# A gated recurrence and a gated long convolution on one core: the same 2430 operations, issued from another order table

## The chip, the core and the metric

The kernel runs on one core of a Trainium2 chip. A core has five engines that each work through their own list of instructions in order: TensorE (PE, matmuls; its weight loads are shown as PEld), VectorE (DVE), ScalarE (ACT), GpSimd (POOL) and SyncE (SP). In this kernel SP does no arithmetic: it issues every DMA. The engines meet only at semaphores, so an instruction whose input or buffer is not ready holds up everything behind it on its own engine.

The metric is the device time of one execution in microseconds (us). Of the kernel before there are three runs: 461.68, 462.61 and 464.66 us, median 462.61.

## What is computed

Four sequences of 6272 steps with 256 channels go through a gated recurrence, and its result through a gated long convolution with a learned filter. Cut to what matters:

```python
def _attn_ref(x, f_logit, lower_bound):
    sig = 1.0 / (1.0 + np.exp(-f_logit))
    f = lower_bound[None, None, :] + (1.0 - lower_bound[None, None, :]) * sig
    i = 1.0 - f
    h = np.zeros((B, D), dtype=np.float32)
    for t in range(S):
        h = f[:, t] * h + i[:, t] * x[:, t]
        y[:, t] = h
    return y

def _moe_ref(x, w_proj, filter_fft, w_out):      # x is the y of above
    proj = x @ w_proj
    x1, x2, x3 = (proj[..., :D].copy(), proj[..., D:2 * D].copy(), proj[..., 2 * D:].copy())
    X2 = np.fft.rfft(x2, n=S, axis=1)
    H = np.fft.rfft(filter_fft, n=S, axis=0)[None, :, :]
    x2_conv = np.fft.irfft(X2 * H, n=S, axis=1)
    y = x1 * x2_conv * x3
    return y @ w_out
```

Batch is 4, S is 6272 = 49 * 128, D is 256; inputs and output are float32.

## The kernel before

The kernel is written as a recording and a replay. The code walks through the computation once and records 2430 operations with `plan.op`: for each one its kind, the engines that may do it (the keys of its cost), the function that issues it, and what it reads and writes. `Plan.emit` then issues them in the order and on the engine that a constant string, `ORDER`, lists. Three characters of that string are one entry: a number in base 64 whose low three bits choose PSUM banks, whose next three bits name the engine (`ENGINES`; MUL is VectorE doing the copy and the following product in one instruction), and whose rest is the operation's number. "A0g", for example, is 3360 = 52 * 64 + 4 * 8 + 0: operation 52, on SP. The planner that made the table is not part of the kernel. The costs, the transfer times `dma` and `lag` and the constant `MARGIN = 1.0` that stand in the calls of `op` are what it is told; they are not read at run time.

The work falls into these stages. The names are the kinds of the operations, the lines are those of the profile.

- Start, once. The filter is loaded in 13 pieces (`ff`, L610), copied (`fr`), turned by TensorE (`rot`, L621), copied (`f2`) and taken through a two-step Fourier transform (`FF1` L646, `afs`, `FF2` L664, `hw`). The spectrum H is stored to DRAM (`hst`, L673). Dummy matmuls (`warm`, L591) stand where the table puts them. The first recurrence runs alongside.
- Recurrence of one batch (`hgrn`), 13 chunks of 512 steps. `load` (L321) brings 512 KB of f_logit into FL and 512 KB of x into XT; there are NX = 3 buffers of each. Then `sig` (L324, ACT), `u` (L326, POOL), and for each half of the channels `su` (L338, transposes on PE), `f` (L351 on ACT or L353 on DVE), `scan` (L359, DVE) into HA, and `wrap`: a copy of a part of HA to another part, 128 KB for a full chunk, on POOL (L293), ACT (L281) or as a DMA on SP (L291).
- P stage: TensorE projects HA (`P`, L705), and `x2` copies the result into X2, on ACT (L281) or DVE (L286).
- Spectrum of one batch, 16 units: `F1` (L718), `A` (copy to HA's other part), every fourth unit `mini` (L734) and `zm` (L740), `F2` (L777), then two products with the spectrum, either directly out of PSUM on DVE (`prod`, L798) or as a copy (L281) and a product on POOL (`pm`, L807), `slot` (L782, POOL), and back: `I2` (L817) and `Th` (copy). The piece of H that a unit needs is loaded by `H` (L755) into one of NH = 3 buffers, unless it is still there.
- Gate: `x13` (L387, PE) projects HA once more. `xs` copies the result to x1s (ACT L283, DVE L288) and x3s (ACT L281, DVE L286), and `z` multiplies them on POOL (L417), or DVE multiplies directly out of PSUM (L408).
- Output: `I1` (L851, PE), `y` (L857, DVE), `proj` (L869, PE), `o` (copy to one of NO = 3 buffers osb, ACT L283 or DVE L288) and `store` (L879).

The table interleaves these: while the spectrum and the output of one batch run, gate work of the same batch and the recurrence of the next batch stand between them. A P stage needs the whole recurrence of its batch, and the first `F1` needs the whole P stage. So TensorE's list has a repeating shape: a P stage of some 13 us, then a long mixed stage of some 85 us from the first `F1` (L718) of a batch to the first `P` (L705) of the next.

The copies out of PSUM may run on ACT or DVE (`either`); the table chooses one of them for each. This is the loop that replays it:

```python
            word = a * 4096 + b * 64 + c
            yield word // 64, self.ENGINES[word // 8 % 8], word % 8
...
        for i, e, b in self.order():
            o = self.ops[i]
            assert e in o["cost"] and i not in seen and o["preds"] <= seen
...
            o["fn"](*args)
```

## Time and profile before

| | before |
|---|---|
| three runs, us | 461.68, 462.61, 464.66 |
| span of the profiled execution, us | 460.2 |
| VectorE busy | 412.1 us, 90% |
| ScalarE busy | 402.7 us, 88% |
| GpSimd busy | 310.2 us, 67% |
| moved by DMA | 121.40 MB, 264 GB/s on average |

The profile is of one execution. Its page begins with the busy time of each engine, then shows the span in 40 slices of 11.5 us, in tenths of busy time. The granted TensorE clock is at 90% or more in all slices but the second:

```profile
DVE  8689998899999996998999996999999987999872
ACT  6799988799999997899999988999998868989663
POOL 6889766188999643778898435789996603857400
PEclk9899999999999999999999999999999999999999
```

The dips of DVE and POOL are the P stages. Transfers are read in the list of DMA issues; its last column is the median time from issue to landing in us:

```profile
Hu<-H SPq DMA_DIRECT2D x55, 512.0 KB, 4.4
FL<-in_f_logit_dram SPq DMA_DIRECT2D x48, 512.0 KB, 5.4
XT<-in_x_dram SPq DMA_DIRECT2D x48, 512.0 KB, 5.5
out_dram<-osb SPq DMA_DIRECT2D x48, 512.0 KB, 4.3
```

Two cautions for reading it. The ends of matmuls are modelled, so a busy TensorE is not a TensorE at its peak. And an engine's instructions overlap: on ACT and DVE the next one starts a little before the profile shows the end of the last one, so what an instruction costs its engine is the distance from its start to the next start, where nothing idles between them.

### The profile page before, as it was taken

The numbers are of one execution on the slowest core, as the hardware profiler recorded it, in microseconds if no ns is written. First come the engines' busy times: TensorE is split into PE (matmuls) and PEld (weight loads), VectorE is DVE, ScalarE is ACT, GpSimd is POOL, SyncE is SP. The second block draws the span as 40 slices with busy tenths as digits, with TensorE's granted clock in tenths as the row PEclk, the third lists the DMA queues.
The fourth block names the chain that finished last, engine by engine and source line by source line (L and its number), as shares of the span: only waits on it lengthen the run. The fifth ranks groups of instructions, "written<-read, shape, count | busy, mean of one in ns | idle before, by whom it ended". The sixth has DMA issues, their size and how long they took to land.

```text
span 460.2 us, 14622 instructions
## 1 busy us (share of the span) xinstructions
PE 439.7 (96%) x6009; PEld 344.3 (75%) x6009; DVE 412.1 (90%) x471; ACT 402.7 (88%) x582; POOL 310.2 (67%) x293
## 2 busy tenths in 40 slices
PE   7799989999989999999999999999999999999997
PEld 5677778766756889778667889767768897777786
DVE  8689998899999996998999996999999987999872
ACT  6799988799999997899999988999998868989663
POOL 6889766188999643778898435789996603857400
PEclk9899999999999999999999999999999999999999
DMA  8967898986997997386887996579869830756176
GB/s 333 390 268 288 315 307 283 349 284 219 309 353 250 358 315 276 139 246 218 307 300 280 318 317 239 214 248 318 255 235 315 306 138 13 230 200 205 57 287 275
DMA packets 44242, 121.40 MB, mean 264 GB/s; under 512 B 4240, under 2 KB 6672, under 8 KB 44176
## 3 DMA queue, kind: packets, MB, share of 16 engines
q1 hardware_dynamic: 44176, 120.47, 74.0%
q8 instruction: 47, 0.77, 0.7%
q14 instruction: 19, 0.16, 0.1%
HBM read 87.69 MB, written 31.98 MB: 260 GB/s over the span
## 4 chain that ended last, share of the span: by engine, by line
PE 63%; DVE 12%; ACT 11%; DMA 5%; issue 5%; POOL 2%; SPq 0%; DVEq 0%; ACTq 0%; POOLq 0%
PE PS L387 14%; PE PS L817 8%; PE PS L869 7%; PE PS L338 7%; PE PS L705 6%; PE PS L777 6%; PE PS L718 5%; DVE HA L359 5%; PE PS L851 4%; DMA FL<-in_f_logit_dram 3%; DVE ys L857 2%; DVE X L286 2%; ACT FL L324 2%; PE PS L646 2%; ACT fTs L351 1%
## 5 line engine op out<-in xcount | busy, mean ns | idle before, releaser
L326 POOL TENSOR_TENSOR XT<-XT,FL 128x1024 f32<-128x1024 f32 (+1 forms) x52 | 116.9, 2251 | 50.3 <-ACT FL L324 41.9
L359 DVE TENSOR_TENSOR_SCAN HA<-fTs,HA,PS 128x512 f16<-128x512 f32 (+1 forms) x96 | 112.5, 1200 | 2.8 <-ACT fTs L351 1.7
L798 DVE TENSOR_TENSOR PP<-PS,Hu 98x1008 f16<-98x1008 f32 x87 | 101.3, 1197 | 3.4 <-ACT HA L281 1.4
L387 PE MATMUL PS<-HA,W 128*128 128x490 f16 (+1 forms) x416 | 100.4, 367 | 0.9 <-DVE X L286 0.4
L807 POOL TENSOR_TENSOR PP<-HA,Hu 98x1008 f16<-98x1008 f16 x41 | 86.2, 2107 | 1.7 <-PE PS L817 1.0
L281 ACT CAST HA<-PS 128x1024 f16<-128x1024 f32 (+1 forms) x94 | 77.0, 849 | 5.1 <-PE PS L718 3.4
L417 POOL TENSOR_TENSOR zt<-x1s,x3s 128x490 f16<-128x490 f32 (+1 forms) x43 | 52.3, 1222 | 41.8 <-ACT x3s L281 22.9
L857 DVE TENSOR_TENSOR ys<-PS,zt 128x1024 fp32r<-128x1024 f32 (+1 forms) x52 | 58.5, 1149 | 9.5 <-PE PS L851 5.0
L283 ACT ACTIVATE osb<-PS 128x1024 f32<-128x1024 f32 (+1 forms) x51 | 49.9, 992 | 13.9 <-PE PS L869 11.2
L351 ACT ACTIVATE fTs<-PS,nomc 128x512 f32<-128x512 f32 (+1 forms) x89 | 58.3, 679 | 3.7 <-PE PS L338 2.3
L387 PEld LDWEIGHTS <-W 128*128 128x128 f16 x416 | 35.4, 97 | 31.7 <-issue 5.4
L869 PE MATMUL PS<-Wo,ys 128*128 128x256 f32 x392 | 57.7, 292 | 1.3 <-DVE ys L857 1.1
L283 ACT ACTIVATE x1s<-PS 128x490 f32<-128x490 f32 (+1 forms) x92 | 53.5, 594 | 5.0 <-PE PS L387 3.0
L817 PEld LDWEIGHTS <-PP 98*128 98x128 f16 x1024 | 48.7, 98 | 10.6 <-issue 3.1
L324 ACT ACTIVATE FL<-FL 128x1024 f32<-128x1024 f32 (+1 forms) x52 | 53.0, 1026 | 2.2 <-DMA FL<-in_f_logit_dram 2.1
L869 PEld LDWEIGHTS PS<-Wo,ys 128*128 128x128 f32 x392 | 49.4, 188 | 5.8 <-DVE ys L857 2.2
L817 PE MATMUL PS<-VA,PP 98*128 98x98 f16 x512 | 52.2, 207 | 1.5 <-ACT x1s L283 0.8
L817 PE MATMUL PS<-VB,PP 98*128 98x98 f16 x512 | 51.9, 207 | 0.0
L281 ACT CAST Th<-PS 128x784 f16<-128x784 f32 x58 | 48.2, 830 | 2.6 <-PE PS L817 1.6
L338 PE MATMUL PS<-iden,FL 64*128 64x64 f32 x784 | 44.8, 230 | 1.6 <-DVE HA L359 0.9
L705 PE MATMUL PS<-W,HA 128*128 128x256 f16 x392 | 44.4, 273 | 1.0 <-ACT X L281 1.0
L705 PEld LDWEIGHTS <-HA 128*128 128x128 f16 x392 | 42.9, 142 | 1.9 <-issue 1.3
(113 smaller groups left out, 724.3 us busy)
## 6 DMA issues: line engine op xcount, KB each, us to landing
Hu<-H SPq DMA_DIRECT2D x55, 512.0 KB, 4.4
FL<-in_f_logit_dram SPq DMA_DIRECT2D x48, 512.0 KB, 5.4
XT<-in_x_dram SPq DMA_DIRECT2D x48, 512.0 KB, 5.5
out_dram<-osb SPq DMA_DIRECT2D x48, 512.0 KB, 4.3
X<-in_moe_filter_fft_dram SPq DMA_DIRECT2D x9, 512.0 KB, 7.1
H<-Hu SPq DMA_DIRECT2D x4, 512.0 KB, 6.2
Hu<-in_moe_filter_fft_dram SPq DMA_DIRECT2D x2, 512.0 KB, 9.8
H<-Hu SPq DMA_DIRECT2D x4, 256.0 KB, 6.5
```

The source lines that it names most:

```text
L281: nc.scalar.copy(dst, src)
L283: nc.scalar.activation(dst, src, AF.Copy, scale=scale)
L326: op("u", {"POOL": 0.1 + 0.553 * nb}, lambda e, xt=xt, ft=ft: nc.gpsimd.tensor_tensor(xt, xt, ft, op=AOP.mult), r=[("ft", k)], w=[("xt", k)])
L338: nc.tensor.transpose(bank(pb)[:, at[p] + j:at[p] + hn:nb], src[ps, j, cols], iden[ps, ps])
L359: nc.vector.tensor_tensor_scan(h, fT, bank(pb)[:, 512 - hn:512 + hn], init, op0=AOP.mult, op1=AOP.add),
L387: nc.tensor.matmul(PS[:, p, 0:n], W13[:, kh, js], HA[:, HB[kh] + t0:HB[kh] + t0 + n], start=(kh == 0), stop=(kh == 1))
L705: nc.tensor.matmul(pp[:, r - r0, :], column(HB[kh], q_of(r)), W2[:, kh, :], start=(kh == 0), stop=(kh == 1))
L798: nc.vector.tensor_tensor(pr, px.unsqueeze(1).broadcast_to([TB, 2, UE, 63]), hh, op=AOP.mult)
L807: nc.gpsimd.tensor_tensor(pr, spec[:, o, :, 1:64].unsqueeze(1).broadcast_to([TB, 2, UE, 63]), hh, op=AOP.mult)
L817: nc.tensor.matmul(PS[:, ib + o, pr * TB:(pr + 1) * TB], PP[:TB, k, o, n, 2 * pr:2 * pr + 2, :], v[:TB], start=(n == 0), stop=(n == 1))
L857: nc.vector.tensor_tensor(late["ys"][:, yk, :, 0:rn * 128], PS[:, cb:cb + 2, 0:rn * 128], late["zt"][:].rearrange("p k r m -> p k (r m)") ...
L869: nc.tensor.matmul(po[:, i, :], late["ys"][:, yk, kh, i * 128:(i + 1) * 128], Wo[:, kh, :], start=(kh == 0), stop=(kh == 1))
```

## The change

Only the constant `ORDER` differs. The recorded operations, buffers, costs and dependences are the same code; the new table was planned with transfer times that one in ten transfers of the trace exceeds, in place of those in the code. The string is two lines shorter in the file, because its lines are longer, so every line below it moves up by two (L326 becomes L324 and so on). The first lines of both tables:

```diff
 ORDER = (
-    "A0gA1AA5gA6AA+gBDgBIgBNgBSgAAYAOYABIACIAPIApQAdQAzYAqQAoQAkQAyQARIA2QA/YA4AA3AAQAAVYAXYBXgAhSAlSBhgBAQBJYBCAAUIA"
-    "WIAfSBBIA7SBEAAvUBcgBFUBOYBGEBHEAiWBKWBTYBLGBrgBMGBPUBREBYYAnWASABmgA9CA8KBwgBZWBiIBUQBdYBbOBVIBQEBjSBsYBlCBaGAT"
...
+    "AAYA0gA5gAOYABIAnUACIBDgApSA+gAiUBNgAyUBIgAzYAPIAlWBXgBSgAfXAkSAoXAvTAdRBhgA1AA2WA6YAhQARIAQAA7SBEAA/YA9CBFUA4GBwg"
+    "BAQBGEBOYBcgA8CBrgAVYAxTBHMBmgBJAAXYD5gBBIBPTBCAAUIADgBRDBYYBKQA3OBQDEFgBTYATIBMABZTASABaLBUVD6gBiYBLIERgBWFEGgBbL"
...
```

Read entry by entry, the two tables issue the same 2430 operations. On TensorE the order, dummy matmuls aside, is nearly kept: an operation moves by 0.4 places on average and by at most 7 of 738. These counts of operations by engine differ:

| kind | before | after |
|---|---|---|
| xs, copies of the gate | ACT 131, DVE 16, MUL 61 | ACT 121, DVE 27, MUL 60 |
| x2, copies of the P stage | ACT 27, DVE 25 | ACT 30, DVE 22 |
| f2 / afs, copies of the start | ACT 19 / 24, DVE 7 / 8 | ACT 15 / 21, DVE 11 / 11 |
| wrap | POOL 34, ACT 8, SP 6 | POOL 26, ACT 4, SP 18 |
| f / o | ACT 89 / 51, DVE 15 / 1 | ACT 88 / 50, DVE 16 / 2 |
| copies before pm | ACT 39, DVE 2 | ACT 38, DVE 3 |
| A / hw | ACT 55 / 14, DVE 9 / 3 | ACT 56 / 15, DVE 8 / 2 |
| fr | POOL 7, ACT 3, DVE 3 | POOL 8, ACT 3, DVE 2 |

The SP list has 263 operations in place of 251, and the loads, spectrum loads, wraps and stores stand in another order in it. The number of direct products (L798, 87) and of `pm` (L807, 41) is the same; `z` on POOL goes from 43 to 44 after one direct product fewer at L408.

126 lines of the change are left out of this document (62 added, 64 removed).

## The prediction

> **What bounds the kernel now.** The busy shares come first, cut to the stages. I take the long mixed stages from the first L718 of a batch to the first L705 of the next. The columns are start and end, length, then busy us of each engine with its instruction count, granted clock, DMA share and GB/s.
>
> ```profile
> core 0: us, PE busy (x) PEld busy (x) DVE busy (x) ACT busy (x) POOL busy (x), PEclk, DMA share, GB/s
> 88.50:172.70 84.20, 80.16 (x1262) 60.31 (x1260) 79.32 (x88) 79.24 (x118) 68.16 (x54) 1.00 0.87 300
> 185.70:273.00 87.30, 85.92 (x1321) 65.42 (x1320) 84.47 (x91) 82.25 (x124) 66.45 (x57) 1.00 0.79 272
> 285.70:371.40 85.70, 84.83 (x1317) 64.80 (x1315) 83.13 (x90) 81.32 (x124) 68.15 (x57) 1.00 0.75 261
> 432.80:460.20 27.40, 24.08 (x331) 20.94 (x330) 15.49 (x14) 13.20 (x14) 0.00 (x0) 1.00 0.64 256
> ```
>
> No engine is alone. In the long stages PE, DVE and ACT are each busy 94 to 99%; only in the output stage at the end are DVE and ACT half idle. So a change that makes nothing cheaper can win only the few per cent of holes. Who makes the holes is read from the chain that ended last. First its shares by engine (page), then the three pieces after the start-up in which it stands still for a DMA (start us, us, what).
>
> ```profile
> PE 63%; DVE 12%; ACT 11%; DMA 5%; issue 5%; POOL 2%; SPq 0%; DVEq 0%; ACTq 0%; POOLq 0%
> 54.92 5.97 DMA FL<-in_f_logit_dram
> 100.43 6.23 DMA Hu<-H
> 125.69 6.87 DMA FL<-in_f_logit_dram
> ```
>
> The DMA's 5% is 23 us, but a piece of the chain is a latency, not a loss: other engines worked meanwhile. What was lost is in the waits (engine and line, waited for: us in total, times, longest one) and, for the spectrum loads, in the L798 group's idle time after the bar.
>
> ```profile
> POOL XT L326 <- DMA XT<-in_x_dram: 2.4, 3, 1.5
> ACT FL L324 <- DMA FL<-in_f_logit_dram: 2.1, 2, 1.2
> ACT osb L283 <- DMA out_dram<-osb: 1.9, 2, 1.7
> L798 DVE TENSOR_TENSOR PP<-PS,Hu 98x1008 f16<-98x1008 f32 x87 | 101.3, 1197 | 3.4 <-ACT HA L281 1.4 <-DMA Hu<-H 1.0 <-PE PS L777 0.4
> ```
>
> That is all a better-timed table can take from the transfers: L324 and L326 wait at the same two places (near 61 and 133 us), so 2.4 + 1.0 in the run plus 1.9 at the end, 5.3 us or 1.2% of the span.
>
> **Part 1, the transfers.** For each load I counted its cover: the PE work that the table puts between the operation that frees the buffer (or an earlier entry of SP's queue that waits longer) and the first operation that uses the data, each PE group at its median distance to the next start (L387 pair 0.41 us, L705 group 0.87, L718 0.45, L777 0.54, L817 0.70, L338 0.60, L869 1.13). It is compared with the landing times: loads of x and f_logit have median 5.5 and one in ten over 8.8 us; spectrum loads 4.4, one in ten over 6.2, the longest 7.5.
> For x and f_logit the cover's least value goes from 4.4 to 5.1 us, the number under 6.2 from 24 to 10 of 104. Around 61 us the picture is mixed: the f_logit load that was late falls from 7.0 to 5.7, the next pair rises from 5.1 to 7.1 and 9.0. Around 133 us the late pair rises from 5.8 and 6.4 to 6.4 and 8.0.
> For the spectrum loads the least value in batch 0 goes from 3.5 to 5.6, but in batches 1 and 2 it falls from 6.4 and 6.9 to 5.8 and 6.0. At the end the five tightest stores have 4.3 to 4.9 before and 4.2 to 5.4 after: nothing is changed there, and I leave the 1.9 us.
> So of 2.4 + 1.0 = 3.4 us I take 2.0 as gained; bounds: gain 5.3, loss 2.0 (the spectrum rival below).
>
> **Part 2, copies from ACT to DVE.** A copy's cost is the distance to the next start, not the busy time. Here in the timeline (start, us, instruction):
>
> ```profile
> 137.75 0.62 ACT L283 ACTIVATE x1s<-PS 128x490 f32<-128x490 f32 x1
> 138.21 0.74 ACT L351 ACTIVATE fTs<-PS,nomc 128x512 f32<-128x512 f32 x1
> 105.25 0.66 DVE L286 COPY x3s<-PS 128x490 f32<-128x490 f32 x1
> 105.82 0.66 DVE L288 TENSOR_SCALAR x1s<-PS 128x490 f32<-128x490 f32 x1
> ```
>
> 138.21 - 137.75 = 0.46 us on ACT, 105.82 - 105.25 = 0.57 on DVE; over all such pairs 0.47 and 0.58. In the same way: 512-column copies of the start 0.48 to 0.53 and 0.60, a 1024-column copy 0.91 and 1.14, an ACT wrap 0.51.
> DVE: 11 xs x 0.58 = 6.4, 7 copies of f2 and afs x 0.60 = 4.2, one each of f, prod-copy and o some 2.0; less 3 x2, one A and one hw x 1.14 = 5.7, one fr 0.65 and one direct gate product 0.57: +5.7. Summed operation by operation, so that small forms count as small, +5.3 (402.5 to 407.8). ACT the same way: -6.9 (383.2 to 376.4), of which xs -4.7 and wraps -2.0.
> Where they lie matters more. Sums by stage, before to after, beside the stage's length:
> - 88.5 to 172.7 (84.2 us): DVE 79.9 to 81.1, ACT 76.8 to 73.4.
> - 185.7 to 273.0 (87.3 us): DVE 83.1 to 86.2, ACT 78.9 to 77.2; PE stays at 83.6.
> - 285.7 to 371.4 (85.7 us): DVE 83.9 to 83.3, ACT 78.5 to 76.0.
> - start: DVE +0.2, ACT -1.3; P stages together: DVE -0.7, ACT +3.9; last batch from 385.2: DVE +2.0, ACT -1.9.
>
> DVE is the fullest engine in the long stages, and the second one gets 3.2 us more where it has 4.2 free. The third stage shows that DVE can fill 83.9 of 85.7 (98%); at that share 86.2 needs 88.0 us, +0.7; at the 95% of the other two it needs 90.7, +3.4. I take +1.2, near the first, because the added copies need not wait for more than their one PE group. The first stage costs nothing at 98% and +1.3 at 95%: zero. What it costs queues behind it: a copy on DVE holds back the scan (L359, 1.19 us) and product (L798, 1.12 us) behind it, and those hold PSUM banks that PE needs.
> ACT is on the chain for 11% of 460.2 = 51 us of its 383, 13%; 13% of -6.9 is -0.9. Bounds: 0 and the whole -6.9.
> The Trainium skill ("Perfetto Trace Analysis", section Optimizing Scalar/DVE Operations) says that where DVE is saturated, moving work from it to Scalar may help; this table goes the other way. By that rule the slower rival below would be the likelier one.
>
> **Part 3, wraps from POOL and ACT to SP.** POOL loses 8 copies and gains one fr and one gate product, net some -2 us; it is on the chain for 2%: zero. SP issues 12 more DMAs:
>
> ```profile
> L293 POOL COPY HA<-HA 128x512 f16<-128x512 f16 x34 | 20.1, 612 | 0.9 <-ACT W L470 0.8
> HA<-HA SPq DMA_DIRECT2D x6, 128.0 KB, 5.0
> ```
>
> One lands after 5.0 us in place of a 0.6 us copy; the shortest cover of the 18 is 5.9 us, the median one over 10, so the consumer is not late. On SP each takes some 0.5 us to issue and may wait for its scan with loads queued behind; that is counted in the covers above. 12 x 128 KB is 1.3% more traffic; the first long stage is at a DMA share of 0.87, so I add +0.4 (bounds 0 and 1).
> In the last stage one full-size o and one small one move to DVE; its 13 y (L857, 1.12 each) fill 14.3 of 27.4 us. Cover: DVE's idle time there. If the copy stands in front of a y that PE waits for, +1.1; taken as zero.
>
> **Sum** against the profiled 460.2: -2.0 + 1.2 - 0.9 + 0.4 = -1.3, so 458.9. The median of the runs lies 2.4 above the span: 461.3 us.
>
> **Rivals.**
> 1. DVE becomes the pace-maker (slower). Both filled-up stages run at 95%: +3.4 and +1.3, the late o +1.1, and no gain from the transfers: 462.6 + 5.8 = 468.4. It decides if DVE keeps its 4 us of holes in the second stage although it has more to do. For it: DVE 12% of the chain, PE waiting behind the scan. Against: the third stage's 98%.
> 2. ACT was the gate (faster). Its savings at the start and in the long stages, 1.3 + 3.4 + 1.6 + 2.5 = 8.8, less 3.9 more in the P stages, come through whole, with 3.4 from the transfers: 462.6 - 8.3 = 454.3; half of it 458.4. For it: all three long stages lose ACT work. Against: ACT has 7 to 8 us free in each of them already.
> 3. The table does not do what it says: the waits were short and stay as they are, 462.6. The three named waits are 1% of the span, and a wait removed for one engine is mostly followed by its next one. The Trainium skill ("DMA: Bandwidth & Descriptors", section Anatomy of one DMA) fits 2.0 us plus bytes over 436 GB/s, on another issue path; as an estimate 3.2 us for 512 KB, with which no cover would be short and the gain nil. The rows say 4.4 to 5.5 us.
> 4. Spectrum loads late in batches 1 and 2. Of their 26 loads one in ten, some three, lands 0.2 to 1.5 us after a cover of about 6: +2, 464.6.
>
> **How the numbers follow.** About 1% (4.6 us) is what a measurement of this kernel can tell from no change; the bounds are 458 and 467.2. Forecast (459 to 464) 0.37; rival 1 0.27; rival 2 0.19; rival 3 0.10; rival 4 0.07. Faster by over 1%: rival 2 and a bit of the forecast, 0.23. Slower: rival 1, 0.27, and 0.02 for a stack of 1 and 4: 0.29. Within: 0.48. The range reaches to rival 1 and to the near half of rival 2: 455 to 469.
>
> **What would show it.** The waits of L324 and L326 (there L322 and L324) on a DMA fall from 2.1 and 2.4 us; the 5.97 and 6.87 pieces leave the chain; L796 (L798 before) does not wait more for Hu. The second long stage, first L716 to first L703, is the longest and its DVE share rises to 97% or more; if it exceeds 90 us, rival 1 is right. If the first and third stages shorten by 2 us or more each, rival 2 is. The forecast would be wrong in kind if the start before the first P group, where I see only +0.2 and -1.3, moved by more than 3 us.

## The result, and the profile after

| | before | after |
|---|---|---|
| median of the runs, us (lowest to highest) | 463.15 (461.68 to 464.66, 4 runs) | 474.75 (473.48 to 477.01, 4 runs) |
| ratio, 95% interval | | 1.0252 [1.0210, 1.0294] |
| span of the profiled execution, us | 460.2 | 472.4 |
| busy: PE, DVE, ACT, POOL, us | 439.7, 412.1, 402.7, 310.2 | 444.4, 418.3, 400.2, 309.0 |

The changed table is 2.5% slower, 11.6 us. The forecast was 461.3, its range 455 to 469. Some executions of a kernel fall in a slower state, more than 1.5% above its fastest one; all times and ratios below are of the others. (A ratio is not the quotient of the two medians and differs from it by up to 0.5%.)

The profile of after answers to the views of before in the same order. First the stages, cut at the same events (start and end, length, busy us of each engine with its instruction count, granted clock, DMA share, GB/s). The first row is the start, up to the first P group; the next three are the long mixed stages; the last is the output stage at the end.

```profile
core 0: us, PE busy (x) PEld busy (x) DVE busy (x) ACT busy (x) POOL busy (x), PEclk, DMA share, GB/s
0.00:79.90 79.90, 66.47 (x705) 52.52 (x706) 68.74 (x106) 65.82 (x94) 60.90 (x84) 0.94 0.89 317
93.10:177.10 84.00, 80.59 (x1259) 60.40 (x1260) 81.10 (x91) 76.91 (x111) 65.11 (x52) 1.00 0.83 273
189.50:278.60 89.10, 86.40 (x1318) 65.16 (x1318) 86.49 (x94) 82.53 (x122) 68.59 (x57) 1.00 0.81 266
291.60:379.90 88.30, 86.21 (x1317) 65.19 (x1315) 84.39 (x92) 80.53 (x119) 66.47 (x53) 1.00 0.78 266
443.00:472.40 29.40, 24.61 (x331) 20.84 (x330) 16.86 (x16) 12.03 (x12) 0.00 (x0) 1.00 0.60 238
```

Read the lengths against those of before: 75.5 for the start, then 84.2, 87.3, 85.7, and 27.4. The changes are +4.4, -0.2, +1.8, +2.6 and +2.0. What is not in these rows: the P stages, whose changes cancel, and the last batch's spectrum, 47.6 to 49.2 us. So there is no one place. VectorE's part can be estimated here: its busy time in the three long stages rises by 1.8, 2.0 and 1.3 us, and its holes (length less busy time) go from 4.9, 2.8 and 2.6 us to 2.9, 2.6 and 3.9. The first stage took its share into the holes; the second is longer by about what VectorE does more in it; the third by twice that. In the last batch's spectrum it is +0.8 busy us (44.84 to 45.66) in a stretch 1.6 longer. If the rises of the last three came through whole, VectorE would account for some 4 of the 12 us; that is an estimate from busy times, not a measurement. In the start it has 9 us of holes before (66.56 of 75.5) and 11 after, so it is not what is short there.

The chain that ended last: its shares by engine, then its longest three pieces, after the start-up, in which it stands still for a DMA (start us, us, what); two more, 5.79 at 135.14 and 5.47 at 209.19, are left out.

```profile
PE 56%; DVE 22%; DMA 8%; ACT 7%; issue 5%; POOL 2%; DVEq 0%; ACTq 0%; POOLq 0%; SPq 0%
```

```profile
160.15 7.09 DMA FL<-in_f_logit_dram
...
264.51 8.36 DMA out_dram<-osb
...
360.84 8.88 DMA FL<-in_f_logit_dram
```

Five pieces in place of three, and the DMA's share is 8% in place of 5%. DVE's share goes from 12% to 22%, ACT's from 11% to 7%. A second profile of the same kernel (after_again, below) has 24% for DVE, 5% for ACT and 10% for the DMA. This looks like VectorE as the pace-maker, more than the estimate above allows.

The waits (engine and line, waited for: us in total, times, longest), then the group of direct products with its idle time by releaser:

```profile
POOL XT L324 <- DMA XT<-in_x_dram: 18.4, 6, 9.0
...
ACT osb L281 <- DMA out_dram<-osb: 3.1, 5, 1.5
...
ACT FL L322 <- DMA FL<-in_f_logit_dram: 2.0, 3, 1.4
```

```profile
L796 DVE TENSOR_TENSOR PP<-PS,Hu 98x1008 f16<-98x1008 f32 x87 | 101.5, 1199 | 3.4 <-PE PS L775 1.9 <-DMA Hu<-H 1.0 <-ACT HA L279 0.2
```

In this profile the table planned for late transfers waits longer for transfers: GpSimd's L324 18.4 us for x where it was 2.4, the output copies 3.1 for a store where it was 1.9, and nothing less elsewhere (2.0 for 2.1, 1.0 for 1.0). The 18.4 us look like the finding; they are not. The same kernel in its second profile, span 474.8 us, has

```profile
POOL XT L324 <- DMA XT<-in_x_dram: 4.3, 3, 1.8
```

so this wait differs by 14 us from one execution to the next, and the execution that waited less was not the faster one.

### The profile page after: what moved, and what is told of

Its sections match the earlier page's. It is cut to its first block, busy times and chain, and to the rows that moved or that the text cites. A ratio compares the mean times of both kernels' runs of the same rounds, so it can differ in the third digit from the quotient of the medians.

```text
span 472.4 us, 14653 instructions
## 1 busy us (share of the span) xinstructions
PE 444.4 (94%) x6009; PEld 346.3 (73%) x6009; DVE 418.3 (89%) x485; ACT 400.2 (85%) x563; POOL 309.0 (65%) x287
## 4 chain that ended last, share of the span: by engine, by line
PE 56%; DVE 22%; DMA 8%; ACT 7%; issue 5%; POOL 2%; DVEq 0%; ACTq 0%; POOLq 0%; SPq 0%
PE PS L385 12%; PE PS L703 8%; DVE HA L357 8%; PE PS L815 6%; PE PS L336 6%; PE PS L867 5%; DMA FL<-in_f_logit_dram 5%; PE PS L775 4%; PE PS L716 4%; DVE PP L796 3%; PE PS L849 3%; DVE ys L855 3%; PE PS L644 3%; DMA out_dram<-osb 2%; DVE zt L406 1%
## 5 line engine op out<-in xcount | busy, mean ns | idle before, releaser
L324 POOL TENSOR_TENSOR XT<-XT,FL 128x1024 f32<-128x1024 f32 (+1 forms) x52 | 117.0, 2250 | 56.5 <-ACT FL L322 30.9
L796 DVE TENSOR_TENSOR PP<-PS,Hu 98x1008 f16<-98x1008 f32 x87 | 101.5, 1199 | 3.4 <-PE PS L775 1.9
L385 PE MATMUL PS<-HA,W 128*128 128x490 f16 (+1 forms) x416 | 102.9, 367 | 0.5
L415 POOL TENSOR_TENSOR zt<-x1s,x3s 128x490 f16<-128x490 f32 (+1 forms) x44 | 53.5, 1223 | 43.0 <-DVE ys L855 14.7
L281 ACT ACTIVATE osb<-PS 128x1024 f32<-128x1024 f32 (+1 forms) x50 | 48.9, 990 | 19.1 <-PE PS L867 14.1
L349 ACT ACTIVATE fTs<-PS,nomc 128x512 f32<-128x512 f32 (+1 forms) x88 | 57.9, 673 | 4.8 <-PE PS L336 2.7
L279 ACT CAST Th<-PS 128x784 f16<-128x784 f32 x58 | 47.6, 820 | 4.4 <-PE PS L815 3.0
L281 ACT ACTIVATE x1s<-PS 128x490 f32<-128x490 f32 (+1 forms) x83 | 47.9, 584 | 3.3 <-DVE zt L406 1.9
L336 PEld LDWEIGHTS PS<-iden,FL 64*128 64x128 f32 x784 | 33.5, 138 | 16.1 <-DVE HA L357 4.6
```

What stands on the lines that cost most here:

```text
L279: nc.scalar.copy(dst, src)
L281: nc.scalar.activation(dst, src, AF.Copy, scale=scale)
L324: op("u", {"POOL": 0.1 + 0.553 * nb}, lambda e, xt=xt, ft=ft: nc.gpsimd.tensor_tensor(xt, xt, ft, op=AOP.mult), r=[("ft", k)], w=[("xt", k)])
L336: nc.tensor.transpose(bank(pb)[:, at[p] + j:at[p] + hn:nb], src[ps, j, cols], iden[ps, ps])
L385: nc.tensor.matmul(PS[:, p, 0:n], W13[:, kh, js], HA[:, HB[kh] + t0:HB[kh] + t0 + n], start=(kh == 0), stop=(kh == 1))
L796: nc.vector.tensor_tensor(pr, px.unsqueeze(1).broadcast_to([TB, 2, UE, 63]), hh, op=AOP.mult)
```

## The experiments

All kernels keep the recorded operations and change the table alone, unless said otherwise. The diffs show the table decoded: number of the operation, kind, batch, engine, PSUM bank. Ratios are to the kernel before, run beside each on the same chip. Kernels cut together from both tables take a list up to an event from one and what is left from the other.

### Which part of the table: engines, wraps, start

The first four start from the changed table and put one part back.

The start, up to the first P group of batch 0 (order, engines, dummies):

```diff
+52 ff b0 SP bank 0
+53 fr b0 ACT bank 0
+57 ff b0 SP bank 0
+58 fr b0 ACT bank 0
...
 0 iden b0 POOL bank 0
-52 ff b0 SP bank 0
-57 ff b0 SP bank 0
...
```

> The table of after, but all operations that the table of before lists ahead of its first P stage stand in before's order and on before's engines; the rest is after's. The two profiles differ by 12.2 us (460.2 to 472.4), and 4.4 of it is there at the first P group (75.5 to 79.9 us). Theory A (the loss has several places, and the start is one of its own): the first P group is back near 75.5 us and the time falls by 4 to 5 us, to about 470. Theory B (the loss is one of the long stages, where a late start would be caught up by engines that wait anyway): the time falls by less than 2 us, to 473 or more. Theory C (the start is the cause of what comes later too, since the loads of the next batch start late): it falls by 8 us or more.

Measured: 476.33 us, 1.0327 [1.0287, 1.0367]. The time is what Theory B gave, but not for its reason. The first P group starts at 76.5 us in place of 79.9, so 3.4 us come back; but the spectrum of batch 0 then takes 66.0 us in place of 59.5. ScalarE's `A` copies wait 4.6 us there for a spectrum store out of the same buffer that lands only at 95.8 us; TensorE stands still behind them for some 4 us and then has a granted clock of 0.50 from 96 to 100 us. That seam, between a start from one list and a rest laid out for the other, ate the gain; the cut was repeated further on (below).

The dummy matmuls of the start alone, six ahead of the first rotation and the others spread, as before, in place of ten ahead:

```diff
+39 warm b0 PE bank 4
+41 warm b0 PE bank 2
+34 warm b0 PE bank 4
+50 warm b0 PE bank 4
+37 warm b0 PE bank 6
+31 warm b0 PE bank 7
 52 ff b0 SP bank 0
...
-39 warm b0 PE bank 4
...
```

> The table of after, with only the 13 dummy matmul groups of the start at the places among TensorE's other operations where before has them: 6 instead of 10 ahead of the first turned filter piece, the others between the pieces. Theory A (the dummies make the start late: in after the first rot starts at 7.9 us instead of 6.3, and TensorE has half its clock for 10.2 us in place of 3.4): the first rot is back at 6.3 us, half clock lasts about 3.4 us, the first P group comes 2.5 to 4 us earlier than in after, the time is 471 to 472. Theory B (the start is late because the copies f2 and fr stand in another order and on other engines, and half clock follows from that): the first rot moves to 6.3 us, the rest of the start does not, and the time stays at 474 to 475.

Measured: 473.93 us, 1.0273 [1.0220, 1.0327]. First rotation at 6.3 us (7.9 in after), half clock for some 3.4 us, first P group at 78.3 us, 1.6 less than in the first profile of after and 3.1 less than the median of seven profiles with its start (table below). In the time there is nothing that can be told apart. Theory A was right about the clock; the time is that of neither theory.

The wraps of all batches on the engines of before (6 on SP in place of 18):

```diff
-280 wrap b0 SP bank 0
+280 wrap b0 POOL bank 0
...
-316 wrap b0 SP bank 0
+316 wrap b0 POOL bank 0
...
```

> The table of after, with every wrap on the engine that before gives it: 6 on SP, 34 on POOL, 8 on ACT instead of 18, 26 and 4; the places in the table are after's. Theory A (wraps on SP stand in front of loads and share the DMA engines with them; loads of x took 6.5 us instead of 5.5 in the median, and POOL waited 18.4 us for them instead of 2.4): the median landing of XT falls below 6, POOL's wait for XT by 5 us or more, and the time by 3 us or more, to 472 or less. Theory B (stores that stand between the two loads of a pair and wait for their copy are what holds the loads up, and the wraps hardly matter): the wait for XT stays above 13 us and the time is within 1.5 us of 474.8.

Measured: 477.68 us, 1.0348 [1.0305, 1.0392]: slower still, with an interval above that of the changed kernel (it just touches that of the control below). The wait that looked like the finding is gone in it:

```profile
POOL XT L323 <- DMA XT<-in_x_dram: 2.6, 2, 2.0
```

2.6 us in place of 18.4, and the time went up by 3 us: both theories are out. The second profile of after, with its wraps on SP, has 4.3 us, so the short wait can't be put down to the wraps. But a short wait for x goes with no shorter time in either, and putting the wraps back gains nothing in this list.

The copies after the start on the engines of before, so that ScalarE gets back what went to VectorE:

```diff
-412 x2 b0 DVE bank 4
+412 x2 b0 ACT bank 4
...
-406 x2 b0 ACT bank 6
+406 x2 b0 DVE bank 6
...
```

> The table of after, with every copy after the start (xs, x2, f, A, Th, o, the copies before pm, and the gate's direct products) on the engine that before gives it, at after's place. ScalarE gets some 5 us of work back and VectorE loses some 5. Theory A (VectorE, fuller by 5.3 us, sets the pace of the long stages, the slower rival of the prediction): the three long stages, 83.8, 88.3 and 88.7 us in after, go back towards 84.2, 87.3 and 85.7, and the time falls by 3 us or more, to 472 or less. Theory B (the engines were chosen for this order; moving copies back puts them behind others on ScalarE): the time rises by 1 us or more. Theory C (copies do not decide): within 1 us of 474.8.

Measured: 482.60 us, 1.0441 [1.0391, 1.0492], 8 us above the changed kernel, as Theory B said. Its second long stage (same columns):

```profile
193.40:284.70 91.30, 86.44 (x1320) 64.91 (x1318) 84.80 (x91) 84.16 (x125) 66.49 (x55) 1.00 0.78 259
```

VectorE does here what it does in the kernel before, 84.80 us, and has 6.5 us of holes, but the stage is 91.3 us long where the changed kernel needs 89.1 with VectorE at 97%. Taking work off the fullest engine made it slower. The other half was tried in the kernel before: its order, with the copies between ACT and DVE after the start on the engines of the changed table.

```diff
-412 x2 b0 ACT bank 2
+412 x2 b0 DVE bank 2
...
-402 x2 b0 DVE bank 2
+402 x2 b0 ACT bank 2
...
```

> The order of the kernel before, with the copies and rescalings on the engines that the changed table gives them (VectorE +5.3 us of planned time, ScalarE -6.9 us), so the shift of work alone without the new order. Theory A (the loss sits in the order, stage by stage; which engine copies matters only through an order made for it): an order made for other engines loses something, ratio to the kernel before 1.005 to 1.03, and of the loss no more than a third can be put down to VectorE being fuller: its busy share in the second and third long stage stays at or under 96%. Rival D (VectorE's extra work is the loss, and the earlier run in the other direction was slow for its mismatch): ratio 1.02 to 1.03 with VectorE at 97% or more in the long stages.

Measured: 475.99 us, 1.0323 [1.0241, 1.0405], more than the 1.03 that Theory A allowed. The second and third long stage:

```profile
186.60:276.60 90.00, 86.00 (x1323) 65.87 (x1319) 87.11 (x95) 81.18 (x120) 65.79 (x57) 1.00 0.78 262
289.90:377.60 87.70, 85.33 (x1317) 64.77 (x1315) 84.59 (x93) 81.09 (x121) 68.37 (x57) 1.00 0.75 255
```

VectorE is at 96.8% and 96.5%, between what the two theories gave and no fuller than in the kernel before (96.8% and 97.0%). The second stage is again longer by what VectorE does more (2.7 and 2.6 us): there its load may well set the length. But half of the change costs as much as the whole, and giving it back costs 8 us on top. An order and an assignment of engines that were not made for each other lose 8 to 13 us either way, and that hides what the copies cost by themselves, with an order of their own.

### Where: stage by stage

A control first, the changed kernel again, then two kernels that follow the kernel before up to the first P group of batch 1 and of batch 3, and the changed table from there.

```diff
 777 store b0 SP bank 0
+1367 load b2 SP bank 0
 954 P b1 PE bank 2
+956 P b1 PE bank 6
 955 x2 b1 DVE bank 2
-956 P b1 PE bank 6
...
```

> The changed kernel once more, unaltered, beside the hybrids of this call, since the runs of one call share a chip and the runs of before. All theories: 2.1 to 2.9% over before, as measured first, with the loss again in the start (4 to 5 us), in the long stages of batches 1 to 3 (1 to 3 us each) and in the output at the end (about 2 us).

> Everything that before lists ahead of the first P group of batch 1 in before's order and on before's engines, the rest as in after. The earlier hybrid, cut at the first P group of batch 0, had 6.5 us lost at its seam (spectrum loads that waited for spectrum stores); here the seam lies where neither is pending. Theory A (the loss is local and adds up: start 4.4 us, the rest in batches 1 to 3): first P group of batch 1 at about 172.7 us as in before, later stages as long as in after, the time 4 to 5 us below after. Theory B (the later stages make up for an early or a late start): less than 2 us below after. Theory C (most of the later loss comes from the start): 8 us or more below after.

> As before_to_P1, but before's table up to the first P group of batch 3 and only the last batch (no recurrence and no loads of x in it, 64 operations of output and 16 units) from after. Theory A (local): from the first P group to the end 91.5 us as in after (before: 87.5), so 4 us slower than before. Theory B (the last batch is late in after only because its loads, stores or copies come late out of the batch ahead): within 1.5 us of before.

| list of before up to | us | ratio |
|---|---|---|
| (control: none of it) | 474.97 | 1.0267 [1.0224, 1.0310] |
| first P of batch 1 | 470.53 | 1.0177 [1.0131, 1.0222] |
| first P of batch 3 | 465.76 | 1.0071 [1.0038, 1.0104] |
| the end (the kernel before) | 462.87 | 1 |

The steps are 4.4, 4.8 and 2.9 us, in kind as Theory A of both kernels said; each time is good to about 2 us, and no interval overlaps the next. The loss is laid down stage by stage and each part stays where its list is: a better list ahead neither hides nor feeds what comes behind. The lengths from the profiles can be pooled wherever a stretch runs one list or the other with engines and order unaltered (medians; lowest to highest, profiles):

| stretch | list of before, us | list of after, us |
|---|---|---|
| start to first P, batch 0 | 75.2 (73.8 to 76.6, 8) | 81.4 (79.9 to 81.9, 7) |
| batch 1, first P to next first P | 100.3 (100.3 to 102.4, 4) | 101.6 (101.0 to 102.6, 7) |
| batch 2 | 99.2 (98.4 to 100.5, 4) | 101.6 (100.3 to 102.1, 7) |
| batch 3 to last landing | 87.6 (1) | 91.2 (90.6 to 91.9, 6) |

The start and the last batch are clear, though the last has only one profile of the list of before; batches 1 and 2 lie close to what one profile differs from the next. Batch 0 behind its first P loses nothing. The first profile of after was the mildest of its seven: in the medians the start costs 6.2 us, not 4.4.

What the start is like in both lists (same columns, 24 to 30 us; first after, then before_to_P1, whose start is that of before, then the kernel with the dummies of before):

```profile
24.00:30.00 6.00, 5.12 (x25) 4.60 (x23) 2.98 (x5) 4.37 (x6) 1.73 (x2) 0.50 0.68 270
```

```profile
24.00:30.00 6.00, 5.88 (x64) 4.51 (x63) 4.76 (x7) 5.36 (x8) 4.75 (x8) 1.00 0.70 281
```

```profile
24.00:30.00 6.00, 5.75 (x34) 4.76 (x33) 3.66 (x6) 4.91 (x6) 2.54 (x3) 0.73 0.72 288
```

TensorE is busy in all three, but in after at half clock: 25 matmuls where the list of before does 64. That list ran on from here at 1.00. Over the whole start after is at half clock for some 10 us, the other six profiles with its start for 17 to 20 us, those with the start of before for 3.4 us or less there. The kernel with the dummies of before has 3.4 us, all of them in this window, and its first P group at 78.3 us. So in that one profile the dummies' places bring back nearly all of the clock and 3.1 of the 6.2 us. The rest is the order, engines or banks of the rotations and their copies. It was not taken apart further.

### Transfers: loads behind stores, and loads that are late in fact

In the changed table SP's list has stores and wraps ahead of loads whose buffer is free. What one late load does is seen in the timeline of after (start us, us, engine, line, operation; in brackets the idle time before and who ended it):

```profile
360.84 0.33 SPq L319 DMA_DIRECT2D FL<-in_f_logit_dram  x1
```

```profile
369.74 1.06 ACT L322 ACTIVATE FL<-FL 128x1024 f32<-128x1024 f32 x1 [1.40 <-DMA FL<-in_f_logit_dram]
...
370.71 1.25 ACT L349 ACTIVATE fTs<-PS,nomc 128x512 f32<-128x512 f32 x2
...
371.41 2.45 DVE L357 TENSOR_TENSOR_SCAN HA<-fTs,HA,PS 128x512 f16<-128x512 f32 x2 [1.33 <-ACT fTs L349]
...
372.75 0.46 PE L849 MATMUL PS<-ID,Th 64*128 64x128 f16 x10 [1.23 <-DVE HA L357]
```

The load was issued when its buffer came free and flew for 8.9 us. ACT waits 1.40 us at the sigmoid; behind it in ACT's list stands the gate factor of an earlier chunk (L349), which needs nothing of that load. The scan waits 1.33 us for that factor, TensorE 1.23 us for the bank that the scan gives up. One wait for a transfer passes through three in-order lists almost whole.

So the next kernel moves 17 loads ahead of the stores and wraps that stood before them:

```diff
 910 load b1 SP bank 0
+911 load b1 SP bank 0
...
-911 load b1 SP bank 0
...
```

> The changed kernel with SyncE's list altered alone: 17 loads of batches 1 to 3 that stand behind a store or a wrap in the list, though their buffer is free before, are moved ahead of it. Theory A (the loss is spread over in-order waits between the compute engines; loads are only a small part): ratio to the kernel before 1.021 to 1.027, as the changed kernel or up to 2 us below it. Rival E (loads held behind stores on SyncE's queue are what makes the long stages of batches 1 to 3 longer): ratio 1.008 to 1.016, 4 to 8 us off the changed kernel, and GpSimd's wait on the loads of XT back to about 3 us from 18.4.

```profile
POOL XT L323 <- DMA XT<-in_x_dram: 5.7, 4, 3.5
```

Measured: 477.98 us, 1.0334 [1.0279, 1.0389]. The wait is 5.7 us, no less than in the second profile of after, so the move can't be said to have shortened it. At the place shown above TensorE follows its own queue again. The time does not fall; it lies some 3 us above the changed kernel, outside what either theory gave, and why is open. Rival E is out: three profiles of this order with a wait of 2.6 to 5.7 us are no shorter than the one with 18.4.

Then the premise: is a table planned for late transfers the better one when transfers are late? Both kernels get an extra copy of each chunk from DRAM to DRAM on the same queue ahead of each load of x and f_logit. It computes nothing.

```diff
-                op("load", {"SP": 0.46}, lambda e, ...: nc.sync.dma_start(
+                op("load", {"SP": 0.46}, lambda e, ...: load_late(
...
+    def load_late(dst, src):
+        junk = dram.tile(list(dst.shape), F32, name=f"junk{count['junk']}")
+        count["junk"] += 1
+        nc.sync.dma_start(junk, src)
+        nc.sync.dma_start(dst, src)
```

> The kernel before with each load of x and f_logit preceded, on the same queue, by a copy of the same chunk from DRAM to DRAM, so that loads land late; the copies are extra work that no output needs. Loads should land 2 to 4 us later than the median 5.4 us. Theory P (an order made for late loads is right when loads are late): the kernel before loses 2% to 5%, ratio 1.02 to 1.05. Theory A (loads have slack in either order and only the order among the compute engines counts): ratio 1.00 to 1.015.

> The changed kernel with the same extra copies. Theory P (the new order pays once loads are late): it comes within 1% of before_slow or below it. Theory A (a worse order whatever the transfers do): it stays 2% to 3.5% above before_slow, ratio to the kernel before 1.025 to 1.05.

Measured: before_slow 524.24 us, 1.1342 [1.1286, 1.1397]; after_slow 549.21 us, 1.1851 [1.1769, 1.1933]. Landing times (KB each, median us to landing), first of before_slow, then of after_slow:

```profile
FL<-in_f_logit_dram SPq DMA_DIRECT2D x48, 512.0 KB, 8.9
...
XT<-in_x_dram SPq DMA_DIRECT2D x48, 512.0 KB, 9.4
```

```profile
FL<-in_f_logit_dram SPq DMA_DIRECT2D x48, 512.0 KB, 8.7
...
XT<-in_x_dram SPq DMA_DIRECT2D x48, 512.0 KB, 9.6
```

and GpSimd's wait for x in the same two:

```profile
POOL XT L332 <- DMA XT<-in_x_dram: 51.5, 21, 5.6
```

```profile
POOL XT L330 <- DMA XT<-in_x_dram: 84.1, 27, 14.6
```

Loads land some 3.5 us later than in the kernel before, about as late as one in ten did there, and the changed table loses more by it, not less: 549.21 / 524.24 = 1.048. Theory P is out. Theory A said that the kernel before would hardly suffer; that was wrong by far: loads have no slack of that size in either order. Its own 2% to 3.5% for the gap was too little as well. The extra copies also lay 51 MB more on the DMA engines, so this is a test of late loads under heavy traffic; and the mean granted clock fell to 0.968 and 0.946, so part of the price, the larger in after_slow, is TensorE's clock.

### How: the place in a list

If the engines' loads do not matter and each stage loses in its own list, the place of single operations should show. Comparing the start of each operation in before and in before_copies_of_after, the lag jumps by 2.5 us at one point of the last batch and is carried on from there: at the first xs copy of its spectrum, which the changed table runs on ScalarE. This one copy of 0.6 us was moved alone, in the kernel before, in two ways.

Late, at its place in the list, where two A copies stand ahead of it on ScalarE:

```diff
 2055 A b3 ACT bank 2
 2056 F1 b3 PE bank 4
 2058 F1 b3 PE bank 0
 2059 A b3 ACT bank 0
 2239 z b3 POOL bank 0
-2247 xs b3 DVE bank 6
+2247 xs b3 ACT bank 6
 2248 xs b3 MUL bank 7
 2060 F1 b3 PE bank 6
```

> The kernel before with one copy of 0.6 us (the first xs of batch 3's spectrum stage) given to ScalarE instead of VectorE, as the changed table does, and kept at its place in the list, so that on ScalarE it stands behind two A copies that wait for matmuls. Theory Q (the price of a moved copy is the place it gets in an in-order list, and what is lost is not won back later): TensorE's F1 after it starts 1.5 to 2.5 us late in the profile, and the end is 2 to 2.5 us later, ratio 1.003 to 1.007. Rival L (it is the load of the engines that counts, 0.6 us on one and -0.87 us on the other): no change at the end, ratio 0.999 to 1.002, the loss taken up by later slack.

Early, ahead of the two A copies:

```diff
 2054 F1 b3 PE bank 2
-2055 A b3 ACT bank 2
 2056 F1 b3 PE bank 4
 2058 F1 b3 PE bank 0
+2239 z b3 POOL bank 0
+2247 xs b3 ACT bank 6
+2055 A b3 ACT bank 2
 2059 A b3 ACT bank 0
-2239 z b3 POOL bank 0
-2247 xs b3 DVE bank 6
 2248 xs b3 MUL bank 7
```

> The same, the same copy on ScalarE, but ahead of the two A copies in the list. The engines' loads are those of one_copy_late to the nanosecond. Theory Q: the F1 after it is 0.3 to 0.7 us late, the end 0 to 0.7 us, ratio 0.999 to 1.003. Rival L: the same time as one_copy_late, whichever that is.

| | us | ratio | last batch, first F1 to first I1 |
|---|---|---|---|
| one_copy_late | 465.54 | 1.0043 [1.0010, 1.0075] | 50.0 us |
| one_copy_early | 461.84 | 0.9975 [0.9941, 1.0008] | 47.8 us |
| the kernel before | 463.23 | 1 | 47.6 us |

The timeline of one_copy_late at that place (same columns):

```profile
386.57 0.58 ACT L280 ACTIVATE x1s<-PS 128x490 f32<-128x490 f32 x1 [0.49 <-PE PS L384]
...
386.78 1.50 PE L715 MATMUL PS<-D,X 128*128 128x128 f16 x24 [0.30 <-DVE X L283]
387.43 1.93 ACT L278 CAST HA<-PS 128x1024 f16<-128x1024 f32 x2 [0.28 <-PE PS L715]
389.24 0.60 ACT L280 ACTIVATE x1s<-PS 128x490 f32<-128x490 f32 x1
389.87 0.67 DVE L405 TENSOR_TENSOR zt<-PS,x1s 128x490 f16<-128x490 f32 x1 [3.23 <-ACT x1s L280]
389.89 0.38 PE L715 MATMUL PS<-D,X 128*128 128x128 f16 x4 [1.61 <-ACT x1s L280]
```

and of one_copy_early:

```profile
383.77 1.05 ACT L280 ACTIVATE x1s<-PS 128x490 f32<-128x490 f32 x2 [0.50 <-PE PS L384]
...
383.98 1.98 PE L715 MATMUL PS<-D,X 128*128 128x128 f16 x32 [0.30 <-DVE X L283]
384.71 1.93 ACT L278 CAST HA<-PS 128x1024 f16<-128x1024 f32 x2
384.85 0.67 DVE L405 TENSOR_TENSOR zt<-PS,x1s 128x490 f16<-128x490 f32 x1 [1.02 <-ACT x1s L280]
```

Read the x1s rows. In the first, one copy runs at 386.57; the other, whose matmul was long done, stands behind both A copies (L278, 1.93 us) and starts at 389.24. The direct product on VectorE waits 3.23 us for it. The fourth F1 needs both to give up their banks, and TensorE stands for 1.61 us after 24 of 32 matmuls. In the second the two copies run one right behind the other (x2), the product waits 1.02 us, and TensorE goes on through all 32. The engines do the same work in both, to the copy. Rival L is out: the place alone is worth 50.0 - 47.8 = 2.2 us in the stretch, and the two times are 3.7 us apart, intervals just not overlapping. In the profiles 2.8 us lie ahead of the changed place, where the lists are alike, so the stretch is the better measure; but it too is one profile of each, and over the seven profiles of this stretch with the unaltered list of after it goes from 48.6 to 50.0 us. Not all of it stays lost: from the first P group of the batch to the last landing late takes 89.7 us and early 88.3, so 1.4 of the 2.2 us are left.

How finely the order is fitted, two kernels ask with random exchanges of neighbours in the lists of TensorE, ScalarE and VectorE, in either table:

```diff
 393 P b0 PE bank 4
+248 hw b0 ACT bank 0
 394 x2 b0 ACT bank 4
-248 hw b0 ACT bank 0
...
```

> The kernel before with random exchanges of neighbours in the lists from the first P of batch 0 on: 90 on TensorE, 40 on ScalarE, 20 on VectorE, each where no operation needs the other; engines, banks and the start unchanged. That is under half of the pairs that the changed table turns round (261, 80 and 26 among the operations that stay on their engine). Theory S (the table before is a finely fitted point, so that nearly any other order loses): 1% to 4% slower, ratio 1.01 to 1.04. Rival R (orders near it are about as good, and the changed table loses by a few particular places): ratio 0.998 to 1.006.

> The changed kernel with as many random exchanges of the same kind. Theory S (the changed table is already an ordinary point, off the fitted one): it loses clearly less than jitter_before does against its own kernel, under 1% more than the changed kernel, ratio 1.022 to 1.036. If the changed table is as finely fitted to its plan as the one before: it loses as much as jitter_before does, 1% to 4% more, ratio 1.035 to 1.07. Rival R: ratio as the changed kernel, 1.02 to 1.03.

Measured: jitter_before 548.05 us, 1.1823 [1.1745, 1.1901]; jitter_after 550.73 us, 1.1878 [1.1827, 1.1930]. Far outside what any theory gave: 150 exchanges cost 85 us in the one and 76 us in the other. Some of them undo each other; 138 and 134 pairs stand turned in the end, so it is some 0.6 us for each. Engines and banks are untouched here, so this is order alone. Either table is finely fitted, the changed one almost as much as the other. The changed table is not a careless order that loses 2.5%. It is another careful one. Rival R is out; of Theory S only the direction holds, for the kernel before and not for the changed one.

### The last stage

The nine late dummies moved behind the last real matmul:

```diff
 2363 xs b3 MUL bank 5
-28 warm b0 PE bank 4
 2364 z b3 POOL bank 0
...
-45 warm b0 PE bank 5
 2371 y b3 DVE bank 6
...
```

> The table of after with its nine dummy matmul groups of the last output stage and the two P stages ahead of it put behind the last real matmul; nothing else moved. Each takes TensorE 0.43 to 0.6 us. Theory A (the planner put them where it took TensorE to be idle until a store or a product came, and in the run it is not idle, so they hold up the 13 output groups, which take 22.9 us in after and 21.0 in before): the end comes 1.5 to 3 us earlier. Theory B (TensorE does wait there, for y on VectorE, and the dummies fill the wait): less than 0.7 us.

Measured: 476.98 us, 1.0285 [1.0220, 1.0350]; from the first I1 of batch 3 to the last landing 27.5 us in place of 28.4 (26.2 in before). That is 0.9 us, between the two theories: at most a part of it, and nothing in the time.

The two output copies that the changed table runs on VectorE, back on ScalarE:

```diff
 2390 I1 b3 PE bank 4
-2378 o b3 DVE bank 0
+2378 o b3 ACT bank 0
 2385 I1 b3 PE bank 6
...
-2428 o b3 DVE bank 5
+2428 o b3 ACT bank 5
```

> The changed kernel with two copies of the last output stage back on ScalarE, at their places in the list: o of the third group, which in the changed kernel stands on VectorE ahead of the y of the fourth group, and o of the last, small one. Theory Q (a copy ahead of a y in VectorE's list holds up the chain that ends the kernel): from the first I1 of batch 3 to the last landing 0.6 to 1.3 us less than the changed kernel's 28.4 us, ratio to the kernel before 1.021 to 1.026. Rival Z (the forecast's own step, that these copies cost nothing in the tail): 28.2 us or more.

Measured: 475.28 us, 1.0247 [1.0170, 1.0324]; the stretch 28.3 us. VectorE's rows around the copy, first of after, then of this kernel (granted clock 1.00 there in both):

```profile
448.51 1.22 DVE L855 TENSOR_TENSOR ys<-PS,zt 128x1024 fp32r<-128x1024 f32 x1
450.01 1.22 DVE L286 TENSOR_SCALAR osb<-PS 128x1024 f32<-128x1024 f32 x1 [0.28 <-PE PS L867]
451.15 2.34 DVE L855 TENSOR_TENSOR ys<-PS,zt 128x1024 fp32r<-128x1024 f32 x2
```

```profile
454.39 1.21 DVE L854 TENSOR_TENSOR ys<-PS,zt 128x1024 fp32r<-128x1024 f32 x1
456.85 2.36 DVE L854 TENSOR_TENSOR ys<-PS,zt 128x1024 fp32r<-128x1024 f32 x2 [1.24 <-PE PS L848]
```

From one y to the next it is 2.64 us with the copy between them and 2.46 without: in place of the copy VectorE waits 1.24 us for TensorE's I1. The copy stood in a hole. Rival Z, the forecast's zero, is right.

Last, the whole list of before from the first I1 of batch 3 on:

```diff
-2365 I1 b3 PE bank 1
+2365 I1 b3 PE bank 2
+2370 I1 b3 PE bank 6
+1880 store b2 SP bank 0
+2375 I1 b3 PE bank 0
 2363 xs b3 MUL bank 5
-28 warm b0 PE bank 4
...
```

> The changed kernel with the list of the kernel before from the first I1 of batch 3 on, dummies, engines and order. Theory Q (the loss is local to each stage's list): that stretch falls from 28.4 to between 25.8 and 26.8 us and the time by about 2 us, ratio 1.018 to 1.024. Rival (the stretch is long since the stages before leave the engines worse placed): 27.5 us or more.

Measured: 473.79 us, 1.0255 [1.0183, 1.0327]; the stretch 26.9 us, 0.1 outside what Theory Q gave. So some 1.5 of its 2.2 us come from its own list, by one profile; in the time 1 to 2 us of 474 are not resolved. That list has four I1 in a row ahead of the first output matmul; the changed one puts two dummies and that matmul among them, so that the third y starts 1.0 us later, counted from the first I1.

## Why the prediction was wrong, point by point

**The step that failed** is the one at the root of all terms: that a table's cost is the sum of each engine's work per stage, plus the loads whose cover is too short. It had no term for where an operation stands in its engine's in-order list. jitter_before has the sums of the kernel before, operation by operation, and takes 85 us more; one_copy_late and one_copy_early have equal sums and nearly equal covers and differ by 2.2 us in the stretch.

- **The start.** "Start: DVE +0.2, ACT -1.3" stood as a zero; its own alarm was a move of more than 3 us. It moved by 4.4 us in the first profile, by 6.2 in the medians of the profiles and, with the rest of batch 0, by 4.4 us in the times: in the profiles the largest single term. Ten dummies ahead of the first rotation and the reordered rotations were in the table to be read. The list was counted, not walked.
- **Part 1, transfers, -2.0.** Came to nothing. In the first profile two of the named waits stayed (2.0 for 2.1 us, 1.0 for 1.0) and GpSimd's was 18.4; in the second ScalarE's was 0.6 and GpSimd's 4.3, and the time was no better. A wait total of one profile was too loose a number to take 2.0 us from. The flights became longer in both (median 5.7 us for FL and 6.5 for XT, from 5.4 and 5.5), which covers measured against the old landing times could not see. A loss by GpSimd's wait it was not either: the profiles with 2.6 to 5.7 us of it are no shorter.
- **Part 2, VectorE +1.2.** The size of the work was right: +5.3 by the sum, 418.3 - 412.1 = +6.2 busy us. The second long stage was to be 88.5 us and was 89.1, with VectorE at 97.1%, as written: the one long stage that came out as forecast, and before_copies_of_after repeats it. But by stage the work came out otherwise: VectorE's busy time rose by 1.8, 2.0 and 1.3 us where the sums gave 1.2, 3.1 and -0.6. So the second stage came near its 88.5 with less added work than the forecast priced, which is in part luck. The third, where VectorE was to lose work and the forecast was zero, lost 2.6, the most of the three.
- **ScalarE -0.9.** ScalarE's busy time fell by 2.5 us where the sum gave 6.9, its share of the chain from 11% to 7%, and no stage gained by it (the first long one is 0.2 us shorter).
- **Part 3, wraps +0.4.** Not seen, and perhaps wrong in sign within this table: with the wraps of before it is 2.9 us slower (477.68 against 474.75; intervals 1.0305 to 1.0392 and 1.0210 to 1.0294, but 1.0224 to 1.0310 for the control), in a list made for the other wraps.
- **The o copies in the last stage, zero.** Right, and for the reason given: idle time of VectorE.
- **Rival 1 (468.4)** had the right side and half of the size, but its mechanism reaches some 4 us by the estimate from busy times; the rest of the loss lies in the start, in holes that opened, and in the last stage, where VectorE is half idle. The rule of the Trainium skill that was weighed with it ("Perfetto Trace Analysis", section Optimizing Scalar/DVE Operations: offload from a saturated VectorE) finds no support here; moving the copies back cost 8 us, in an order not made for it, so the rule is not refuted. **Rival 2** (ScalarE the gate) is out, since less work there gained nothing. **Rival 3** was right that the transfers' waits would not pay, **rival 4** wrong: L796 waits 1.0 us for Hu as before.

**What is shown, and what is not.** Shown: the loss is local to the start with the rest of batch 0, the middle batches and the last batch (4.4, 4.8, 2.9 us); putting the wraps back gains nothing, and the time does not follow the wait for x; order alone, with engines and banks as they were, can cost far more than this change did, and one operation's place some 2 us where it stands; and the changed order is worse too when loads are late. Argued, not shown: that VectorE's load is about a third of the loss; no run has that load in an order made for it. Untested: the PSUM banks. The changed table gives 567 operations other banks than the table before, and every kernel cut together from both takes them along with the order, so what is called order here is order and banks. Open: which places make up the loss in each stage (one late load is traced, the last stage's list is 1.5 of 2.2 us, the start's clock and order are not taken apart), and why the planner, told of later transfers, chose worse places. The planner is not in the kernel, so a plan with other transfer times was not tried. No version tried is measurably faster than the kernel before; one_copy_early, at 0.9975 [0.9941, 1.0008], can't be told from it.

## What to carry to other kernels

When a change reorders in-order lists whose engines are all over 94% busy, walk the two lists through the stage, operation by operation, and ask of each moved one what it now stands behind; sums per engine and shares of the chain do not see it. Profile a kernel twice before you explain a wait's total: 18.4 us of it were 4.3 in another execution of the same kernel, and the time did not follow, while a copy of 0.6 us in the wrong place cost some 2 in its stretch. In a table this finely fitted a new plan has little idle time to win and much to lose.

## What the runs showed of the hardware

- Where the dummy matmuls stand goes with how long TensorE runs at half clock in the start. Mean granted clock over the span, where nothing but the table was altered and no exchanges were made: 0.978 to 0.989 in seven profiles with the changed start, 0.992 to 1.000 in seven with the start of before (in start_of_before the half clock lies at the seam, behind the start), 0.996 with the changed start and the dummies of before. A mean of 0.989 over 472.4 us is some 10 us at half clock, 0.982 over 474.8 some 17. The places shift the odds and do not settle it: one of the four runs of tail_dummies_last, with the changed start, has 0.996. The Trainium skill ("TensorE: Matmul & The Clock Gate", section Part 1: The HAM clock gate) says that the warm-up is a span of sustained activity, about 3.4 us, and not a number of matmuls. The runs agree in kind: the same number of dummies, placed elsewhere, gave another clock. How long the activity has to last was not tested.
- Extra copies of 512 KB, one directly ahead of each load of x and f_logit, lengthen the flight of these loads the most, from 5.4 to about 9 us. Stores on the same queue went from 4.3 to 6.1 and 7.0, spectrum loads from 4.4 to 4.7.
